# A decode kernel's w1 in one piece, and q's four products summed in the same rows

## The chip, the cores and the metric

The kernel runs on one core of a Trainium2 chip. The metric is the device time of one execution in microseconds, taken over several executions.

## The reference

Two layers, each of attention with a cached K and V and of a gated feed-forward, for four sequences with one token each. The same weights and the same cache serve both layers. Everything is 32 bit floating point.

```python
B, Sq, D = 4, 1, 512;  Hq, Hkv, Sk, Dh = 32, 8, 4096, 128;  F = 1792
def _A_ref(x, k_cache, v_cache, wq, wo):
    q = (x @ wq).reshape(B, Sq, Hq, Dh).transpose(0, 2, 1, 3)
    k, v = jnp.repeat(k_cache, 4, axis=1), jnp.repeat(v_cache, 4, axis=1)
    p = softmax(jnp.einsum("bhqd,bhkd->bhqk", q, k) * (Dh ** -0.5))
    o = jnp.einsum("bhqk,bhkd->bhqd", p, v)
    return o.transpose(0, 2, 1, 3).reshape(B, Sq, Hq * Dh) @ wo
def _B_ref(x, w1, w3, w2):
    return (silu(x @ w1) * (x @ w3)) @ w2
for _ in range(2):
    x = x + _A_ref(layernorm(x), A_k_cache, A_v_cache, A_wq, A_wo)
    x = x + _B_ref(layernorm(x), B_w1, B_w3, B_w2)
```

## The kernel before

All weights and the cache are laid out by the host as one long row per partition, `rows`, in the order in which the first layer uses them: output and query weights (`wo`, `wq`) of a group of heads, the tiles of K and V (`kv`) group by group, then `w1`, `w3` and `w2`. On the chip one buffer, `space`, has 218 units of 1 KB per partition. The table `LOADS` is written out by hand: each entry is (first unit in the stream, number of units, place in `space`). `pump` (L118) issues the entries strictly in order on SyncE's queue, and stops at the first entry whose place is still taken. `done` (L147) is called when a piece has been used for the last time; it frees the units and calls `pump`. So the use of a piece by TensorE is what lets a later load be issued. Some pieces are kept from the first layer for the second: all of `w1`, some `wq` and `wo`, and 28 of the 32 tiles of the last group of heads, with which the second layer begins.

A group of heads is one turn of the loop at the end of `tile_decode_layers`. `score` (L309) multiplies q with the K tiles of half the positions; the four sequences' products go to four blocks of 32 rows of one PSUM bank. Then `maximum` on VectorE, `exponent` on ScalarE, and `turn` (L343), which transposes the probabilities on TensorE. Between `maximum` and `turn`, TensorE forms the next group's q: `share_q` (L290). Its four products, one for each 128 rows of `wq`, go to four separate blocks of 32 rows of the bank `wide`; `take_q` scales all 128 rows; `turn_q` (L302), called from within the second `score`, multiplies each head's columns with `same`, which both adds up the four blocks and turns them: `misc[:, h * B:(h + 1) * B]` gets the head's q with the head dimension along the partitions. `copy_q` puts it into `qT`. `weigh` (L379) is the product with V. In all there are 15 calls of `share_q`; the first q of the second layer comes from `turn_over`.

The feed-forward (L452) has `gate` and `up` in two PSUM banks. The columns F = 1792 are cut into four blocks of 448, one for each 32 rows, and these into a first part of 256 columns, "a", and a second of 192, "b": both `w1` and `w3` are stored as an a-part and a b-part with four chunks of D each. `part` (L456) multiplies one such part, `swish` (L473) is the gate's sigmoid (ScalarE) and product (VectorE), `times_up` the product with `up` (VectorE), `turn_h` the transposes of h, and `down` (L497) the product with `w2`, whose result is added to x in `x_ps`. In the first layer the order is w3a, w1a, swish and times_up of a, w1b, first transposes, swish of b, w3b; in the second w1a, w1b, swish of all, w3a, times_up of a, w3b. `busy` and `hum` are matmuls of the identity that fill waits of TensorE.

A 32 bit matmul shows as two matmul and two weight load instructions in the trace, a transpose as one of each.

Of the kernel before, what the change touches and what calls it, by code (L numbers as in the profile page):

```python
# [8 lines left out]
F32 = mybir.dt.float32  # L9
AF = mybir.ActivationFunctionType  # L10
ALU = mybir.AluOpType
AX = mybir.AxisListType

B, D, HQ, HKV, SK, DH, F = 4, 512, 32, 8, 4096, 128, 1792
LAYERS = 2
REP = HQ // HKV
P = 128
KC = D // P
# [16 lines left out]
FJ = F // 4  # L35
HALF = 256
EPS = 1e-5
SCALE = DH ** -0.5
# [4 lines left out]
KB = 256  # L43
HOME = 8
SPACE = 218
TURN = HKV - 1
KEPT = (*range(2, 16), *range(20, 32))
HELD = 4
# [10 lines left out]
    (868, 8, 68), (876, 8, 186), (884, 8, 194), ("stash", 1, 202), (892, 8, 206), ("stash", 0, 214),  # L59
# [13 lines left out]
def tile_decode_layers(ctx: ExitStack, tc: tile.TileContext, rows, out):  # L73
    nc = tc.nc
    ctx.enter_context(tc.manual_schedule())
    const = ctx.enter_context(tc.tile_pool(name="const", bufs=1))
    work = ctx.enter_context(tc.tile_pool(name="work", bufs=2))
# [22 lines left out]
    for g in range(3, HKV):  # L100
        stream += tiles(g)
    stream += pair(6)
    for kind, n in (("w1a", KC), ("w1b", KC), ("w3a", KC), ("w3b", KC), ("w2", 14)):
        stream += [(kind, k) for k in range(n)]
    size = {"wq": HOME, "wo": HOME, "kv": U // KB, "w2": D // KB}
    for kind in ("w1", "w3"):
        size[kind + "a"], size[kind + "b"] = 4 * HALF // KB, 4 * (FJ - HALF) // KB
    offset, total = {}, 0
    for key in stream:
        offset[key] = total  # L110
# [34 lines left out]
        return place(where[key], size[key[0]])  # L145

    def done(layer, *key):  # L147
        if layer == 0 and (key[0][:2] == "w1" or key[0] in ("wq", "wo") and key[1] >= HELD or key[:2] == ("kv", TURN) and key[2] in KEPT):
            return
        at, n = where[key], size[key[0]]  # L150
        taken[at:at + n] = [False] * n
        pump()
# [4 lines left out]
    ident = const.tile([P, P], F32, name="ident")  # L157
    make_identity(nc, ident)
    same = const.tile([P, 32], F32, name="same")
# [3 lines left out]
    half, share, spare = columns[:, 0:2], columns[:, 2:3], columns[:, 3:4]  # L163
    rowsum, ssq, ve, rstd = columns[:, 4:5], columns[:, 5:6], columns[:, 6:8], columns[:, 8:10]
# [6 lines left out]
    part = work.tile([P, 32], F32, name="part", tag="p", bufs=1)  # L171
# [11 lines left out]
    x_ps, misc = sums_ps[:, 0, :], sums_ps[:, 1, :]  # L183
    wide = sums_ps.rearrange("p k c -> p (k c)")
# [18 lines left out]
    def hum(n):  # L203
        nc.tensor.matmul(sums_ps[:, 1:1 + n, :], ident, ident.unsqueeze(1).to_broadcast([P, n, P]),
                         start=False, stop=False)
# [73 lines left out]
        return xT, factor  # L279


    def copy_q(q=None):
        q = misc[:, 0:B * REP].rearrange("p (h b) -> p b h", h=REP) if q is None else q
        nc.vector.tensor_copy(qT[:, :, LEAD:].rearrange("p b (t r) -> p b t r", t=2)[:, :, :, 0:REP],
                              q.unsqueeze(2).to_broadcast([P, B, 2, REP]))

# [3 lines left out]
    def share_q(layer, g, xT):  # L290
        w = wq_of(g)
        for k in range(KC):
            nc.tensor.matmul(wide[32 * k:32 * k + 32, :], xT[:, 32 * k:32 * k + 32], w[:, k, :],  # L293
                             start=True, stop=True)
        done(layer, "wq", g)

    def take_q(rstd):
        shares = work.tile([P, REP * DH], F32, name="shares", tag="p", bufs=1)
        nc.vector.tensor_scalar(shares, wide, rstd, -D * SCALE, op0=ALU.mult, op1=ALU.mult)  # L299
        return shares  # L300

    def turn_q(shares):  # L302
        for h in range(REP):
            nc.tensor.matmul(misc[:, h * B:(h + 1) * B], shares[:, h * DH:(h + 1) * DH], same[:, 0:B],  # L304
                             start=True, stop=True)

# [142 lines left out]

    def feed_forward(layer, xT, factor):  # L452
        gate, up = o_ps if layer else o_ps[::-1]
        cols = {"a": slice(0, HALF), "b": slice(HALF, FJ)}

        def part(bank, kind, ks=range(KC)):  # L456
            s = cols[kind[2]]
            for k in ks:
                w = loaded(kind, k).rearrange("p (j f) -> p j f", j=4)
                for j in range(4):  # L460
                    nc.tensor.matmul(bank[32 * j:32 * j + 32, s], xT[:, 32 * k:32 * k + 32], w[:, j],  # L461
                                     start=(k == 0), stop=(k == KC - 1))
                done(layer, kind, k)

        def old_x():
            n = 1 if layer else KC
            nc.tensor.matmul(sums_ps[:, 0:n, :], ident, x_sb.unsqueeze(1).to_broadcast([P, n, P]), start=True, stop=False)

        h = work.tile([P, FJ], F32, name="h", tag="p", bufs=1)
        hT = work.tile([P, 14, B], F32, name="hT", tag="pT", bufs=1)  # L470
        pt = scores().rearrange("p (n s) -> p n s", n=NT)

        def swish(s):  # L473
            nc.scalar.activation(h[:, s], gate[:, s], AF.Sigmoid, scale=rstd[:, 0:1])
            nc.vector.scalar_tensor_tensor(h[:, s], gate[:, s], rstd[:, 0:1], h[:, s], op0=ALU.mult, op1=ALU.mult)

        def times_up(s):
            nc.vector.scalar_tensor_tensor(h[:, s], up[:, s], rstd[:, 0:1], h[:, s], op0=ALU.mult, op1=ALU.mult)

        def turn_h(u):  # L480
            if u == 0:
                for i in range(2):
                    nc.tensor.transpose(pt[:, i, :], h[:, i * P:(i + 1) * P], ident)
                nc.vector.tensor_copy(hT[:, 0:8, :],
                                      pt[:, 0:2, :].rearrange("p i (j b) -> p (i j) b", j=4)[:, :, 0:B])
            else:
                nc.tensor.transpose(pt[:, 2, :], h[:, 2 * P:3 * P], ident)
                nc.tensor.transpose(pt[:, 3, :], h[:, FJ - P:FJ], ident)
                nc.tensor.transpose(pt[0:64, 3, :], h[:, FJ - 64:FJ], ident)
                nc.vector.tensor_copy(hT[:, 8:12, :],  # L490
                                      pt[:, 2, :].rearrange("p (j b) -> p j b", j=4)[:, :, 0:B])
                last = pt[:, 3, :].rearrange("p (j u b) -> p j u b", j=2, u=2)
                for i in range(2):
                    nc.vector.tensor_copy(hT[64 * i:64 * i + 64, 12:14, :],
                                          last[64 * i:64 * i + 64, :, i, 0:B])

        def down():  # L497
            for m in range(14):
                t = loaded("w2", m)
                for k in range(KC):  # L500
                    nc.tensor.matmul(x_ps[32 * k:32 * k + B, :], hT[:, m, :], t[:, k * P:(k + 1) * P],  # L501
                                     start=False, stop=(m == 13))
                done(layer, "w2", m)
                if layer == 0 and m in (1, 3, 8, 11):
                    hum(1)
                if m == (1 if layer else 5):
                    turn_h(1)

        if layer == 0:
            part(up, "w3a", (0,))  # L510
            factor()
            part(up, "w3a", range(1, KC))
            old_x()
            part(gate, "w1a")
            swish(cols["a"])
            times_up(cols["a"])
            hum(3)
            part(gate, "w1b")
            turn_h(0)
            swish(cols["b"])  # L520
            nc.scalar.activation(spare, half[:, 0:1], AF.Exp)
            part(up, "w3b", (0, 1))
            hum(2)
            part(up, "w3b", (2, 3))
            times_up(cols["b"])
            hum(1)
        else:
            old_x()
            part(gate, "w1a", (0,))
            factor()  # L530
            part(gate, "w1a", range(1, KC))
            part(gate, "w1b")
            swish(slice(0, FJ))
            part(up, "w3a")
            times_up(cols["a"])
            part(up, "w3b")
            turn_h(0)
            times_up(cols["b"])
        down()

    for layer in range(LAYERS):
        order = orders[layer]
        if layer:
            xT, factor = turn_over(order[0][0])
        else:
            nc.vector.reduce_sum(rowsum, x_sb, axis=AX.X)  # L546
            xT, factor = layernorm()
# [6 lines left out]
        between = {1: factor} if layer else {}  # L554
        for n, (g, (first, last)) in enumerate(order):
# [10 lines left out]
            pT = turn(p)  # L566
            between = {}
            if n + 1 < len(order):
                shares = take_q(rstd[:, 0:1])
                between[2] = lambda shares=shares: turn_q(shares)  # L570
            if layer == 0 and n == TURN - 2:
                between[6] = lambda: center(TURN)
            if n > ready:
# [71 lines left out]
```

## Time and profile before

| | us |
|---|---|
| median of three executions | 703.92 (703.74 to 704.41) |
| profiled execution, its own time | 703.98 |
| its span | 702.2 |
| mean granted TensorE clock | 0.831 |

Busy time is the time in which an engine had at least one instruction of a group running; "mean ns" is the mean duration of one. Where instructions run side by side, the number times the mean is more than the busy time. The idle time behind a second bar is that of the engine just ahead of the group's instructions, with what ended it. In a timeline row the first number is the start and the second the duration, in us. For a DMA issue the last number is the median time from issue to landing, in us.

### The profile page before, as it was taken

What the parts mean: (1) busy time and instruction counts of PE and PEld (TensorE: products, weight loads), DVE (VectorE), ACT (ScalarE), POOL (GpSimd) and SP (SyncE); (2) the same over time, 40 slices, a digit from 0 to 9 for tenths busy, and PEclk for the clock granted to TensorE, in tenths of its full rate; (3) what the DMA queues carried; (4) which work ended last, traced back from release to release, by engine and by line L of the source; (5) the groups of instructions that cost most, each with busy time, mean ns of one, the idle gap of its engine ahead of it and who ended that gap; (6) DMA issues with size and microseconds to landing.
All of it is one profiled execution on the core that took longest, in us unless ns stands there. A gap on an engine that the chain in (4) does not pass through costs nothing.

```text
span 702.2 us, 7492 instructions
## 1 busy us (share of the span) xinstructions
PE 421.1 (60%) x3280; PEld 133.2 (19%) x3280; DVE 144.4 (21%) x512; ACT 41.7 (6%) x100; POOL 3.0 (0%) x10
## 2 busy tenths in 40 slices
PE   1266466444578409667687985745555744567676
PEld 0121121101112102121134221201111211111223
DVE  2012112121023103330221332112120211212231
ACT  0010000100001001010101210000100001000100
POOL 0000000000000000000000000000000000000000
PEclk9997677966769859886999998878977978779999
DMA  9999999999999999999999999999999999999996
GB/s 418 422 419 422 467 419 418 430 454 413 453 413 441 429 434 418 434 427 426 422 416 378 433 421 442 441 434 420 443 437 430 433 427 444 423 433 413 428 424 269
DMA packets 12271, 297.87 MB, mean 424 GB/s; under 512 B 1360, under 2 KB 1488, under 8 KB 4048
## 3 DMA queue, kind: packets, MB, share of 16 engines
q1 hardware_dynamic: 12240, 297.41, 99.0%
q8 instruction: 25, 0.41, 0.2%
q14 instruction: 6, 0.05, 0.0%
HBM read 297.34 MB, written 0.07 MB: 424 GB/s over the span
## 4 chain that ended last, share of the span: by engine, by line
DMA 73%; PE 23%; DVE 1%; another core or an unknown queue 1%; ACT 1%; issue 1%; SPq 0%; ACTq 0%; DVEq 0%
DMA space<-in_rows 73%; PE scores L320 11%; PE o L385 7%; PE sums_ps L304 1%; PE turned L346 1%; ACT p L339 1%; DVE acc L333 1%; PE scores L200 1%; PE stored L249 1%; PE o L461 0%; PE stored L439 0%; PE sums_ps L418 0%; PE sums_ps L429 0%; PE sums_ps L293 0%
## 5 line engine op out<-in xcount | busy, mean ns | idle before, releaser
L320 PE MATMUL scores<-space,qT 128*32 128x512 f32 x1024 | 166.7, 702 | 136.2 <-DMA space<-in_rows 135.5
L385 PE MATMUL o<-space,pT 128*16 128x512 f32 x1024 | 153.7, 713 | 102.7 <-DMA space<-in_rows 95.9
L320 PEld LDWEIGHTS scores<-space,qT 128*32 128x32 f32 x1024 | 35.5, 122 | 213.2 <-issue 174.2
L385 PEld LDWEIGHTS o<-space,pT 128*16 128x16 f32 x1024 | 31.7, 108 | 202.8 <-DMA space<-in_rows 98.0
L333 DVE TENSOR_REDUCE acc<-scores 128x1 f32<-128x512 f32 x32 | 22.1, 691 | 177.5 <-PE scores L320 177.5
L339 ACT ACTIVATE p<-scores,acc 128x512 f32<-128x512 f32 x30 | 20.6, 687 | 559.8 <-DVE acc L333 433.1
L408 DVE SCALAR_TENSOR_TENSOR o<-o,acc,o 128x128 f32<-128x128 f32 x112 | 39.3, 351 | 50.1 <-PE o L385 46.7
L348 DVE COPY pT<-turned 128x256 f32<-128x256 f32 x32 | 13.6, 424 | 161.9 <-PE turned L346 161.9
L346 PE MATMUL turned<-ident,p 128*128 128x128 f32 x128 | 22.7, 304 | 11.9 <-ACT p L339 11.9
L293 PE MATMUL sums_ps<-space,xT 128*32 128x512 f32 x120 | 23.5, 731 | 3.6 <-DMA space<-in_rows 3.6
L346 PEld LDWEIGHTS turned<-ident,p 128*128 128x128 f32 x128 | 14.7, 151 | 45.4 <-ACT p L339 25.8
L419 DVE COPY o<-sums_ps 128x16 f32<-128x16 f32 x16 | 2.8, 174 | 92.9 <-PE sums_ps L418 92.9
L304 PEld LDWEIGHTS sums_ps<-same,shares 128*128 128x128 f32 x120 | 15.6, 204 | 16.1 <-DVE shares L299 11.9
L304 PE MATMUL sums_ps<-same,shares 128*128 128x4 f32 x120 | 17.0, 265 | 0.9 <-DVE shares L299 0.9
L461 PE MATMUL o<-space,xT 128*32 128x192 f32 (+1 forms) x256 | 13.7, 355 | 3.1 <-DMA space<-in_rows 1.4
L439 PE MATMUL stored<-space,o 128*32 128x512 f32 x104 | 13.5, 592 | 0.0
L501 PE MATMUL sums_ps<-space,hT 128*4 128x128 f32 x224 | 9.1, 272 | 4.2 <-DMA space<-in_rows 3.5
L299 DVE TENSOR_SCALAR shares<-sums_ps,columns 128x512 f32<-128x512 f32 x15 | 11.1, 742 | 1.7 <-PE sums_ps L293 1.7
L209 PE MATMUL o<-columns,same 128*32 128x1 f32 x64 | 2.0, 181 | 14.5 <-DVE columns L546 13.5
L418 PEld LDWEIGHTS sums_ps<-columns,o 128*128 128x128 f32 x32 | 6.2, 240 | 20.3 <-issue 13.5
L461 PEld LDWEIGHTS o<-space,xT 128*32 128x32 f32 x256 | 7.8, 110 | 8.2 <-DVE xT L222 1.4
L418 PE MATMUL sums_ps<-columns,o 128*128 128x16 f32 x32 | 7.6, 315 | 0.6 <-DVE o L408 0.6
(101 smaller groups left out, 141.5 us busy)
## 6 DMA issues: line engine op xcount, KB each, us to landing
space<-in_rows SPq DMA_DIRECT2D x11, 4096.0 KB, 22.1
space<-in_rows SPq DMA_DIRECT2D x7, 2048.0 KB, 27.8
space<-in_rows SPq DMA_DIRECT2D x13, 1024.0 KB, 20.2
space<-in_rows SPq DMA_DIRECT2D x2, 6144.0 KB, 30.8
space<-in_rows SPq DMA_DIRECT2D x2, 5120.0 KB, 28.8
space<-in_rows SPq DMA_DIRECT2D x2, 4608.0 KB, 22.1
space<-in_rows SPq DMA_DIRECT2D x1, 7680.0 KB, 34.0
space<-in_rows SPq DMA_DIRECT2D x2, 3584.0 KB, 20.9
```

The source lines that it names most:

```text
L293: nc.tensor.matmul(wide[32 * k:32 * k + 32, :], xT[:, 32 * k:32 * k + 32], w[:, k, :], start=True, stop=True)
L304: nc.tensor.matmul(misc[:, h * B:(h + 1) * B], shares[:, h * DH:(h + 1) * DH], same[:, 0:B], start=True, stop=True)
L320: nc.tensor.matmul(ps[32 * b:32 * b + 32, :], qT[:, b, at:at + 32], t[:, i * BLOCK:(i + 1) * BLOCK], start=(m < 2), stop=(m >= TILES - 2))
L333: nc.vector.tensor_reduce(acc[:, i:i + 1], ps, axis=AX.X, op=ALU.max, negate=True)
L339: nc.scalar.activation(p.rearrange("p n s -> p (n s)"), ps, AF.Exp, bias=acc[:, i:i + 1], scale=1.0 if scale is None else scale, accum_out ...
L346: nc.tensor.transpose(pt[:, n, :], p[:, n, :], ident)
L348: nc.vector.tensor_copy(pT, pt.rearrange("p n (b r) -> p n b r", b=B)[:, :, :, 0:ROW])
L385: nc.tensor.matmul(o_ps[i][32 * b:32 * b + ROW, :], pT[:, r // 2, b, :], t[:, j * NB * DH:(j + 1) * NB * DH], start=(r < 2), stop=(r >= TI ...
L408: nc.vector.scalar_tensor_tensor(o, o_ps[s][:, j * DH:(j + 1) * DH], acc[:, 16 + NB * s + j:17 + NB * s + j], o, op0=ALU.mult, op1=ALU.add)
L418: nc.tensor.matmul(misc[:, 0:B * REP], o, head, start=True, stop=True)
L439: nc.tensor.matmul(bank[32 * h:32 * h + 32, :], oT[:, h, :], w[:, h, :], start=first, stop=last)
L461: nc.tensor.matmul(bank[32 * j:32 * j + 32, s], xT[:, 32 * k:32 * k + 32], w[:, j], start=(k == 0), stop=(k == KC - 1))
```

## The change

`w1` is stored as four whole chunks of 7 units instead of an a-part and a b-part; its two loads of 16 and 12 units become 21 and 7, at the same places. The first layer's feed-forward takes w1 whole, and its swish runs over all 448 columns; what follows is reordered. The four products of `share_q` are summed in PSUM in the first 32 rows; `take_q` scales 32 rows; `turn_q` turns each head with a transpose; `copy_q` reads with another stride.

```diff
-    (1180, 16, 146), (1152, 16, 0), (1168, 12, 16), (1196, 6, 140), (1202, 6, 146), (1208, 4, 158),
+    (1180, 16, 146), (1152, 21, 0), (1173, 7, 21), (1196, 6, 140), (1202, 6, 146), (1208, 4, 158),
...
-    for kind, n in (("w1a", KC), ("w1b", KC), ("w3a", KC), ("w3b", KC), ("w2", 14)):
+    for kind, n in (("w1", KC), ("w3a", KC), ("w3b", KC), ("w2", 14)):
...
-    def copy_q(q=None):
-        q = misc[:, 0:B * REP].rearrange("p (h b) -> p b h", h=REP) if q is None else q
+    def copy_q():
+        q = misc.rearrange("p (h b) -> p b h", h=REP)[:, 0:B, :]
...
-            nc.tensor.matmul(wide[32 * k:32 * k + 32, :], xT[:, 32 * k:32 * k + 32], w[:, k, :],
-                             start=True, stop=True)
+            nc.tensor.matmul(wide[0:32, :], xT[:, 32 * k:32 * k + 32], w[:, k, :],
+                             start=(k == 0), stop=(k == KC - 1))
...
-        nc.vector.tensor_scalar(shares, wide, rstd, -D * SCALE, op0=ALU.mult, op1=ALU.mult)
+        nc.vector.tensor_scalar(q, wide[0:32, :], rstd[0:32, :], SCALE, op0=ALU.mult, op1=ALU.mult)
...
-            nc.tensor.matmul(misc[:, h * B:(h + 1) * B], shares[:, h * DH:(h + 1) * DH], same[:, 0:B],
-                             start=True, stop=True)
+            nc.tensor.transpose(misc[:, 32 * h:32 * h + 32], q[:, h * DH:(h + 1) * DH], ident[0:32, 0:32])
...
-            part(gate, "w1a")
-            swish(cols["a"])
+            hum(3)
+            part(gate, "w1")
+            swish(cols["1"])
+            nc.scalar.activation(spare, half[:, 0:1], AF.Exp)
             times_up(cols["a"])
-            hum(3)
-            part(gate, "w1b")
+            part(up, "w3b", (0, 1))
             turn_h(0)
-            swish(cols["b"])
-            nc.scalar.activation(spare, half[:, 0:1], AF.Exp)
-            part(up, "w3b", (0, 1))
-            hum(2)
+            hum(1)
             part(up, "w3b", (2, 3))
             times_up(cols["b"])
             hum(1)
         else:
             old_x()
-            part(gate, "w1a", (0,))
+            part(gate, "w1", (0,))
             factor()
-            part(gate, "w1a", range(1, KC))
-            part(gate, "w1b")
-            swish(slice(0, FJ))
+            part(gate, "w1", range(1, KC))
+            swish(cols["1"])
```

More of the change, by code (lines that the diff above doesn't have):

```diff
@@ L102, in tile_decode_layers @@
     stream += pair(6)
-    for kind, n in (("w1a", KC), ("w1b", KC), ("w3a", KC), ("w3b", KC), ("w2", 14)):
+    for kind, n in (("w1", KC), ("w3a", KC), ("w3b", KC), ("w2", 14)):
         stream += [(kind, k) for k in range(n)]
     size = {"wq": HOME, "wo": HOME, "kv": U // KB, "w2": D // KB}
-    for kind in ("w1", "w3"):
-        size[kind + "a"], size[kind + "b"] = 4 * HALF // KB, 4 * (FJ - HALF) // KB
+    size["w1"], size["w3a"], size["w3b"] = F // KB, 4 * HALF // KB, 4 * (FJ - HALF) // KB
     offset, total = {}, 0
@@ L147, in done @@
     def done(layer, *key):
-        if layer == 0 and (key[0][:2] == "w1" or key[0] in ("wq", "wo") and key[1] >= HELD or key[:2] == ("kv", TURN) and key[2] in KEPT):
+        if layer == 0 and (key[0] == "w1" or key[0] in ("wq", "wo") and key[1] >= HELD or key[:2] == ("kv", TURN) and key[2] in KEPT):
             return
@@ L292, in share_q, with turn_q @@
         for k in range(KC):
-            nc.tensor.matmul(wide[32 * k:32 * k + 32, :], xT[:, 32 * k:32 * k + 32], w[:, k, :],
-                             start=True, stop=True)
+            nc.tensor.matmul(wide[0:32, :], xT[:, 32 * k:32 * k + 32], w[:, k, :],
+                             start=(k == 0), stop=(k == KC - 1))
         done(layer, "wq", g)
     def take_q(rstd):
[L298 to L302, printed above, removed]
+        q = work.tile([P, REP * DH], F32, name="shares", tag="p", bufs=1)[0:32, :]
+        nc.vector.tensor_scalar(q, wide[0:32, :], rstd[0:32, :], SCALE, op0=ALU.mult, op1=ALU.mult)
+        return q
+    def turn_q(q):
         for h in range(REP):
-            nc.tensor.matmul(misc[:, h * B:(h + 1) * B], shares[:, h * DH:(h + 1) * DH], same[:, 0:B],
-                             start=True, stop=True)
+            nc.tensor.transpose(misc[:, 32 * h:32 * h + 32], q[:, h * DH:(h + 1) * DH], ident[0:32, 0:32])
     def score(layer, g, c, between={}):
@@ L453, in feed_forward @@
         gate, up = o_ps if layer else o_ps[::-1]
-        cols = {"a": slice(0, HALF), "b": slice(HALF, FJ)}
+        cols = {"1": slice(0, FJ), "a": slice(0, HALF), "b": slice(HALF, FJ)}
         def part(bank, kind, ks=range(KC)):
-            s = cols[kind[2]]
+            s = cols[kind[-1]]
             for k in ks:
@@ L568, in tile_decode_layers @@
             if n + 1 < len(order):
-                shares = take_q(rstd[:, 0:1])
-                between[2] = lambda shares=shares: turn_q(shares)
+                q = take_q(rstd[:, 0:1])
+                between[2] = lambda q=q: turn_q(q)
             if layer == 0 and n == TURN - 2:
@@ L632 @@
     parts = [wog[0], wog[1], wqg[1], wqg[0], old.reshape(P, P), kv[0], *pair(2), kv[1], kv[2], *pair(4), *kv[3:], *pair(6),
-             *halves(w1), *halves(w3), full, rest]
+             chunks(w1), *halves(w3), full, rest]
     parts = [a.reshape(P, -1) for a in parts]
```

## The prediction

> **What bounds the kernel now.** I read the page first: busy shares, slices, queues, and the chain that ended last.
>
> ```profile
> PE 421.1 (60%) x3280; PEld 133.2 (19%) x3280; DVE 144.4 (21%) x512; ACT 41.7 (6%) x100; POOL 3.0 (0%) x10
> DMA  9999999999999999999999999999999999999996
> q1 hardware_dynamic: 12240, 297.41, 99.0%
> q8 instruction: 25, 0.41, 0.2%
> HBM read 297.34 MB, written 0.07 MB: 424 GB/s over the span
> DMA 73%; PE 23%; DVE 1%; another core or an unknown queue 1%; ACT 1%; issue 1%; SPq 0%; ACTq 0%; DVEq 0%
> ```
>
> TensorE is busy in 60% of the span; the 16 DMA engines have work in every slice but the last, and the load queue alone takes 99.0% of their time. The span is therefore a fixed 297.41 MB at the rate of the engines, plus a start and a tail. The 23% of the chain that fall to PE are not a second bound: the chain goes through the PE instruction that consumed a load, while the next loads were already moving. An edit to PE work changes the time only where it makes the queue run dry, where it lengthens the tail after the last landing, or where it changes the traffic itself.
>
> So the second reading is how far the queue runs ahead of the loads. These are issue-to-landing times: the first load of the kernel (the queue is empty), the usual large ones, and then the small ones of 350 to 400 us and of 370 to 382 us, where the first layer's feed-forward gives back its slots piece by piece.
>
> ```profile
> space<-in_rows SPq DMA_DIRECT2D x1, 4160.0 KB, 12.4
> space<-in_rows SPq DMA_DIRECT2D x11, 4096.0 KB, 22.1
> ...
> space<-in_rows SPq DMA_DIRECT2D x1, 3072.0 KB, 13.3
> space<-in_rows SPq DMA_DIRECT2D x7, 512.0 KB, 6.0
> ```
>
> 4160 KB at 424 GB/s are 10.0 us, so an unqueued load costs 2.4 us beside its bytes. A load of 4096 KB alone would take 9.9 + 2.4 = 12.3 us and takes 22.1: it can be issued 9.8 us later before an engine idles. For the 3072 KB load (units 908 to 932, the only one of that size between 350 and 400 us) this reserve is 13.3 - 7.4 - 2.4 = 3.5 us; for the 512 KB loads of 370 to 382 us it is 6.0 - 1.2 - 2.4 = 2.4 us. These three reserves are what every delay below is held against.
>
> The third reading is the tail.
>
> ```profile
> 670.64 15.79 SPq L138 DMA_DIRECT2D space<-in_rows  x7
> ...
> 697.54 1.71 PE L501 MATMUL sums_ps<-space,hT 128*4 128x128 f32 x32 [0.55 <-DMA space<-in_rows]
> 699.31 0.29 DVE L597 COPY space<-sums_ps 128x128 f32<-128x128 f32 x1 [5.01 <-PE sums_ps L501]
> 699.63 0.35 SPq L598 DMA_DIRECT2D out<-space  x1
> ```
>
> The last loads were issued by 686.4, and the w2 rows at 697.54 still wait for them: over 10 us of queue. After them come only a copy and the store. The change touches none of this.
>
> **The change part by part.** First q's products. `share_q` issues eight instructions of 128x512 (four products of two passes) in each of its 15 calls, `turn_q` eight of 128x4.
>
> ```profile
> L293 PE MATMUL sums_ps<-space,xT 128*32 128x512 f32 x120 | 23.5, 731 | 3.6 <-DMA space<-in_rows 3.6
> L249 PE MATMUL stored<-space,columns 128*128 128x512 f32 x8 | 3.7, 605 | 0.0
> L304 PE MATMUL sums_ps<-same,shares 128*128 128x4 f32 x120 | 17.0, 265 | 0.9 <-DVE shares L299 0.9
> L346 PE MATMUL turned<-ident,p 128*128 128x128 f32 x128 | 22.7, 304 | 11.9 <-ACT p L339 11.9
> ```
>
> 120 x 731 ns are 87.7 us, but the group is busy for 23.5: the four products, each in its own 32 rows, run side by side, and a call takes 1.57 us. Summed in the same rows they must follow one another. The nearest row is L249, also four products accumulated in one place: eight instructions in 3.7 us. The upper bound is 8 x 731 ns = 5.8 us. So a call costs 2.1 to 4.3 us more; I take 2.1, since L249 has the same lengths and order. `turn_q` falls from 17.0 / 15 = 1.13 us to four transposes. Those of L346, four times wider, take 22.7 / 32 = 0.71 us for four: 0.4 us less, perhaps 0.7. Net 1.4 to 3.9 us more per call, 21 to 59 us of PE in all. That is the sign opposite to the instruction count.
>
> The Trainium skill, page "TensorEngine Tiling (Array Packing)", section Theoretical Speedup, allows up to 4 times for a stationary side of at most 32 columns; here the trace shows 87.7 / 23.5 = 3.7 before, and the change gives it up. By that rule alone a call would cost 4 x 1.57 = 6.3 us, 4.7 us more, and 15 calls 71 us of PE.
>
> What hides it: the 9.8 us of reserve behind the large loads, in every group but one. PE is made late once per group and then waits again for a landing, so the delays do not add up; a group has 702 / 16 = 44 us, of which PE uses 26. The exception is the first group of the second layer, which runs on kept tiles.
>
> ```profile
> 388.52 1.04 PE L293 MATMUL sums_ps<-space,xT 128*32 128x512 f32 x8
> 390.77 0.66 PE L346 MATMUL turned<-ident,p 128*128 128x128 f32 x4 [1.21 <-ACT p L339]
> 393.19 1.05 PE L304 MATMUL sums_ps<-same,shares 128*128 128x4 f32 x8
> ```
>
> Here the call is 1.04 us and PE then waits 1.21 us for p. With 3.7 us the transposes of p start about 3.7 - 1.04 - 1.21 = 1.4 us later; 0.3 to 0.4 come back in `turn_q`. With 5.8 us it is 3.5. What is queued behind on PE are the second scores, whose last tiles release the 3072 KB load. 1.1 us late against 3.5 us of reserve costs nothing; at the upper bound, 3.2, still nothing.
>
> The multiplication and copy of q on DVE keep their column counts, and so their durations; fewer rows gain nothing that a row here shows. The column sums drop out with -D and `same`.
>
> Next, w1 in one piece. Bytes and number of loads stay. Only a boundary moves: 16 and 12 KB per partition become 21 and 7, issued by SP at the same two places. The first lands 5 x 128 KB / 424 GB/s = 1.5 us later, the second where it did.
>
> ```profile
> L461 PE MATMUL o<-space,xT 128*32 128x256 f32 x128 | 7.8, 381 | 1.3 <-DVE xT L222 1.1 <-DMA space<-in_rows 0.2
> L461 PE MATMUL o<-space,xT 128*32 128x192 f32 x128 | 6.2, 329 | 1.8 <-DMA space<-in_rows 1.2 <-DVE h L478 0.6
> 385.94 2.76 PE L320 MATMUL scores<-space,qT 128*32 128x512 f32 x24
> 368.90 1.51 PE L461 MATMUL o<-space,xT 128*32 128x192 f32 x32 [0.79 <-DMA space<-in_rows]
> 370.70 0.86 PE L461 MATMUL o<-space,xT 128*32 128x192 f32 x16
> 372.59 0.86 PE L461 MATMUL o<-space,xT 128*32 128x192 f32 x16 [0.40 <-DMA space<-in_rows]
> 373.94 0.62 PE L501 MATMUL sums_ps<-space,hT 128*4 128x128 f32 x16
> 377.21 0.40 PE L501 MATMUL sums_ps<-space,hT 128*4 128x128 f32 x8 [0.72 <-DMA space<-in_rows]
> ```
>
> Half of each L461 row is w1: (7.8 + 6.2) / 2 = 7.0 us in both layers. By L320 a 448 wide instruction is 2.76 / 24 x 448 / 512 = 0.10 us, and 64 of them are 6.4 us: 0.3 us less per layer, on a path that waits for landings.
>
> The order in the first layer matters more. Now both halves of the sigmoid and its product stand ahead of the first half's multiplication by up, and the last part of w3 comes right behind that. The second layer already runs so:
>
> ```profile
> 688.40 0.63 ACT L474 ACTIVATE h<-o,columns 128x448 f32<-128x448 f32 x1 [19.98 <-PE o L461]
> 689.07 0.68 DVE L475 SCALAR_TENSOR_TENSOR h<-o,columns,h 128x448 f32<-128x448 f32 x1 [3.16 <-ACT h L474]
> 690.05 0.48 DVE L478 SCALAR_TENSOR_TENSOR h<-o,columns,h 128x256 f32<-128x256 f32 x1 [0.29 <-PE o L461]
> 690.59 1.51 PE L461 MATMUL o<-space,xT 128*32 128x192 f32 x32 [0.61 <-DVE h L478]
> ```
>
> The last row says that w3's last columns wait until DVE has read the other columns of the same bank. So in the first layer: w1 ended at 370.4; the second load still lands just ahead of 368.90, and what follows it, one piece of eight instructions and the end of the one before, brings w1's end to about 369.9. Then 0.63 + 0.68 + 0.48 and about 0.2 of hand-overs give 371.9 for the first two pieces of w3b, which ran at 370.70: 1.2 us late. Queued behind it on PE are the transposes of h, the other two pieces, and w2, about 1.1 us late at 373.9; the two 512 KB loads and their neighbours that go into these slots are issued as late. Against a reserve of 2.4 us that is nothing, and at 377.21 PE waits for a landing again, so it is back on time. If the bank's wait did not occur, the delay would be 0; the bounds of this term on the time are 0 and, should the reserve be used up by the engine that runs ahead, 1 us. I take 0. The order of the filling matmuls changes inside these waits: nothing.
>
> In the second layer the feed-forward has 0.3 us less PE work ahead of w2, whose last loads are waited for: nothing. The loads that go into w1's first slot are issued about 0.3 us later, since its first piece is now 448 wide; against the 10 us of queue at the end that is nothing.
>
> Last, the traffic. 25 instruction packets took 0.2% of 16 x 702.2 us, about 22 us or 0.9 each (0.41 MB / 25 = 16 KB). Each holds one DMA engine while the others go on, so it delays the landings only if that engine is the last. 252 TensorE instructions fewer are about one packet: between 0 and 0.9 us less; spread over 16 engines 0.06. I take 0. That the remaining packets fall at other times, onto other moments of the queue, can move the end by one packet either way.
>
> **Sum.** 0 (q, hidden) + 0 (order, hidden) + 0 (w1) + 0 (packets) on the profiled execution's 703.98 us (span 702.2 and 1.8 around it), which is 0.06 above the median of the three times: 704.0 us. About 0.2%, or 1.4 us, is what a measurement of this kernel can tell from no change.
>
> **The rivals.** *Instruction packets make it faster.* The last DMA engine loses one or two packets that now fall on others: 0.9 or 1.8 us less, 702.2 for two. For it: the queue is never empty, so an engine's lost time is never won back but in the stretch of small loads. Against: only one packet in 25 goes. The Trainium skill, page "Runtime: NRT & Kernel Launch", section Instruction fetch mechanics, says that instructions come in blocks of 256, 16 KiB, through a DMA queue of the engine's own; the size of a packet here agrees.
>
> *The stretch of small loads runs dry, and it becomes slower.* The place is 371 to 377 us in the first feed-forward: w3b waits for DVE, the slots of w3b and w2 come free late. It decides from 2.4 us of delay on. My estimate is 1.2; were the hand-overs and the extra transposes double, 3.5 to 4, the loads would come 1.1 to 1.6 us late, and a packet on the wrong engine could add 0.9: 705.1 to 706.5 us. For it: this is the smallest reserve in the kernel, and it is a median, so single loads have less. Against: the landings re-time PE within 4 us.
>
> *The products do not serialize.* If one row group overlaps its own products after all, PE gets lighter; the time stays 704.0 because PE does not bound it.
>
> **How the numbers follow.** No change, with either behaviour of the products, 0.56. Faster by the packets 0.20. Slower by the dry stretch 0.24, for which the small reserve speaks. The range goes from two packets less to the dry stretch with 1.6 us: 702.2 to 705.6.
>
> **What would show it.** Right: the load queue again near 99.0%, the last w2 still waiting for DMA, L293's group near 55 us instead of 23.5 with its mean below 731 ns, the transposes of q below 11 us, 24 instruction packets. Wrong: a dip of the DMA digits or GB/s between 370 and 400 us well below those of before, loads of 512 KB that land in under 4 us from issue, or a w2 at the end that waits for PE.

## The result, and the profile after

The changed kernel takes 706.66 us (median of 17 executions, 704.43 to 711.6) against 703.92 us (17 executions, 703.54 to 704.62): ratio 1.0047, 95% interval 1.0032 to 1.0063. It is slower by about 3 us, and its times scatter over 7 us where the kernel before scatters over 1. Each ratio below is to the kernel before, run beside that experiment. In three of the experiments one execution took 1274 to 2196 us, in a slow state, and is left out of every figure. The profiled execution took 710.18 us (span 708.4), 3.5 us above its median; its differences from before are larger than the typical ones.

From the page of the changed kernel:

```profile
PE 451.1 (64%) x3156; PEld 131.5 (19%) x3156; DVE 144.2 (20%) x511; ACT 41.4 (6%) x99; POOL 3.0 (0%) x10
GB/s 418 414 415 470 415 419 446 432 422 438 426 433 432 442 419 424 438 426 426 414 419 353 368 423 431 443 449 414 431 455 415 434 434 421 449 433 406 425 423 224
q1 hardware_dynamic: 12240, 297.41, 98.4%
q8 instruction: 25, 0.41, 0.2%
HBM read 297.34 MB, written 0.07 MB: 420 GB/s over the span
DMA 69%; PE 27%; DVE 1%; another core or an unknown queue 1%; issue 0%; SPq 0%; ACT 0%; ACTq 0%
```

The same bytes went at 420 instead of 424 GB/s. The two slices with 353 and 368 lie between 372 and 407 us; before, the slices of this place had 378 and 433. There the load queue ran short; elsewhere the slices look as before.

The groups that the change touches (by line, shapes kept apart):

```profile
L292 PE MATMUL sums_ps<-space,xT 128*32 128x512 f32 x120 | 63.6, 681 | 3.4 <-DMA space<-in_rows 3.4
L303 PE MATMUL sums_ps<-ident,shares 32*128 32x32 f32 x60 | 6.4, 227 | 0.9 <-DVE shares L298 0.9
L459 PE MATMUL o<-space,xT 128*32 128x448 f32 x64 | 6.5, 542 | 2.1 <-DMA space<-in_rows 1.7 <-DVE xT L221 0.3
```

The products of q run one after another: 120 x 681 ns are 81.7 us for 63.6 of busy time, where before the ratio was 3.7. A call takes 4.2 us instead of 1.57.

The first feed-forward and the second layer's start, in the timeline:

```profile
366.96 3.21 PE L459 MATMUL o<-space,xT 128*32 128x448 f32 x32 [1.74 <-DMA space<-in_rows]
371.70 0.48 DVE L476 SCALAR_TENSOR_TENSOR h<-o,columns,h 128x256 f32<-128x256 f32 x1
372.24 0.86 PE L459 MATMUL o<-space,xT 128*32 128x192 f32 x16 [2.06 <-DVE h L476]
393.32 3.60 PE L292 MATMUL sums_ps<-space,xT 128*32 128x512 f32 x8
```

w1 now waits for its larger first load (366.96), and q's products in the second layer's first group take 3.60 us instead of 1.04. The first two pieces of w3b start at 372.24 instead of 370.70, behind VectorE's read of the same bank. The load that goes into their slots is issued later. These are the answers for the one 512 KB load issued there, of before (window from 371.4 us) and of after (window from 373.0 us):

```profile
space<-in_rows SPq DMA_DIRECT2D x1, 512.0 KB, 5.6
```

```profile
space<-in_rows SPq DMA_DIRECT2D x1, 512.0 KB, 4.1
```

Now the DMA digits of the window 370 to 382 us, 0.3 us each, of before and then of after:

```profile
DMA  8999999999899989997999999996887998999989
```

```profile
DMA  9999999999764996799999959799999999999999
```

Each digit is the busy share of the 16 engines in tenths. Before, the engines are nearly full through the stretch (lowest digit 6, at 378 us); after, there is a hole from 373.0 to 375.1 us, just where the refill is late. And by stretches (length; busy PE, PEld, DVE, ACT, POOL; granted clock; DMA share; GB/s), before first:

```profile
370.00:376.00 6.00, 5.39 (x86) 2.93 (x77) 0.94 (x3) 1.91 (x3) 0.00 (x0) 1.00 1.00 374
382.00:392.00 10.00, 7.64 (x125) 3.30 (x126) 3.16 (x12) 3.29 (x8) 0.70 (x1) 1.00 1.03 419
392.00:405.00 13.00, 12.48 (x108) 4.09 (x106) 5.24 (x22) 1.10 (x3) 0.00 (x0) 1.00 1.03 432
```

```profile
370.00:376.00 6.00, 3.94 (x68) 2.43 (x68) 1.78 (x4) 2.12 (x3) 0.00 (x0) 1.00 0.91 337
382.00:392.00 10.00, 8.87 (x106) 4.25 (x110) 1.77 (x8) 0.37 (x2) 0.70 (x1) 0.50 1.00 376
392.00:405.00 13.00, 13.00 (x94) 3.80 (x88) 3.56 (x11) 4.03 (x9) 0.00 (x0) 0.99 0.95 353
```

Three things went wrong in a row in this execution: the DMA hole at 373 us; a granted clock of 0.50 through 382 to 392 us; and a second hole behind it, 353 instead of 432 GB/s, in the second layer's first group, where TensorE waits for no load and its pace decides when slots come free. Which of them is the cause, the experiments had to say.

### The profile page after: what moved, and what is told of

It reads as the page before. It is cut to its first block, busy times and chain, and to the rows that moved or that the text cites. A ratio compares the mean times of both kernels' runs of the same rounds, so it can differ in the third digit from the quotient of the medians.

```text
span 708.4 us, 7238 instructions
## 1 busy us (share of the span) xinstructions
PE 451.1 (64%) x3156; PEld 131.5 (19%) x3156; DVE 144.2 (20%) x511; ACT 41.4 (6%) x99; POOL 3.0 (0%) x10
## 3 DMA queue, kind: packets, MB, share of 16 engines
q1 hardware_dynamic: 12240, 297.41, 98.4%
## 4 chain that ended last, share of the span: by engine, by line
DMA 69%; PE 27%; DVE 1%; another core or an unknown queue 1%; issue 0%; SPq 0%; ACT 0%; ACTq 0%
DMA space<-in_rows 69%; PE scores L318 11%; PE o L383 8%; PE sums_ps L292 4%; PE turned L344 1%; PE o L459 1%; PE stored L248 1%; PE sums_ps L303 1%; PE sums_ps L499 0%; DVE pT L346 0%; PE scores L259 0%; PE stored L437 0%; DVE o L406 0%; PE sums_ps L203 0%
## 5 line engine op out<-in xcount | busy, mean ns | idle before, releaser
L292 PE MATMUL sums_ps<-space,xT 128*32 128x512 f32 x120 | 63.6, 681 | 3.4 <-DMA space<-in_rows 3.4
L292 PEld LDWEIGHTS sums_ps<-space,xT 128*32 128x32 f32 x120 | 14.3, 124 | 48.1 <-issue 42.8
L459 PE MATMUL o<-space,xT 128*32 128x256 f32 (+2 forms) x192 | 13.4, 417 | 6.5 <-DMA space<-in_rows 3.3
L298 DVE TENSOR_SCALAR shares<-sums_ps,columns 32x512 f32<-32x512 f32 x15 | 10.9, 729 | 6.0 <-PE sums_ps L292 6.0
L459 PEld LDWEIGHTS o<-space,xT 128*32 128x32 f32 x192 | 5.8, 109 | 12.6 <-DVE h L476 4.9
L303 PEld LDWEIGHTS sums_ps<-ident,shares 32*128 32x128 f32 x60 | 4.8, 136 | 14.8 <-DVE shares L298 11.9
```

Of the source, the lines that this page charges most:

```text
L292: nc.tensor.matmul(wide[0:32, :], xT[:, 32 * k:32 * k + 32], w[:, k, :], start=(k == 0), stop=(k == KC - 1))
L303: nc.tensor.transpose(misc[:, 32 * h:32 * h + 32], q[:, h * DH:(h + 1) * DH], ident[0:32, 0:32])
```

## The experiments

At first I held the clock to be the cause, and q's serial products to be the rival. Unless another is named, "the hole" is the one from 373 us on.

**The w1 part alone.** Edit: the kernel before with the changed `LOADS`, stream and `feed_forward`, and the old `share_q`, `take_q`, `turn_q`, `copy_q`.

> Before, with the w1 part of the change alone (w1 in one piece, the new order of the first feed-forward); q's products stay in four row groups. Theory clock (the new order leaves TensorE idle in the first feed-forward, its clock falls to half around 382 us, and the first group of the second layer, which paces the loads, runs at half speed): some executions slower by 2 to 5 us, spread of the times over 2 us, median 705 to 706; a profile of a slow one shows clock 0.5 between 380 and 392 us. Theory serial q (the summed products make TensorE late in that group): 703.5 to 704.3 with the narrow spread of before, clock 1.0 in that stretch.

705.45 us (704.36 to 707.51), ratio 1.0026, interval 1.0016 to 1.0037. Over half of the loss is here, without any change to q. The clock was at 0.5 for only 3.4 us in this profile; the hole is there (window 370 to 382 us):

```profile
DMA  9999999875646977999989965799999999999999
```

**The q part alone.**

```diff
-            nc.tensor.matmul(wide[32 * k:32 * k + 32, :], ..., start=True, stop=True)
+            nc.tensor.matmul(wide[0:32, :], ..., start=(k == 0), stop=(k == KC - 1))
```

with the new `take_q`, `turn_q` and `copy_q`, and nothing of w1.

> Before, with the q part of the change alone (products summed in 32 rows, heads turned by transposes); w1 and the first feed-forward as before. Theory clock: 703.7 to 704.8, narrow spread, clock 1.0 between 360 and 420 us, the L293 group at some 60 us busy. Theory serial q: nearly all of the loss, 706 to 707, with DMA below 0.97 busy between 395 and 410 us.

703.96 us (703.51 to 711.35, one of eleven above 704.3), ratio 1.0008, interval 0.9989 to 1.0026. The profile is from a second run:

> The q part of the change alone once more, for a profile: 703.5 to 704.3; DMA digits of 370 to 382 us full, the L293 group at some 60 us busy with a mean below 731 ns, its transposes below 11 us.

704.04 us (703.5 to 706.88), ratio 1.0004, interval 0.9994 to 1.0015. TensorE is busier by 21 us, and that costs nothing that can be measured: the load queue hides it.

```profile
PE 442.1 (63%) x3220; PEld 130.9 (19%) x3220; DVE 144.3 (21%) x512; ACT 41.7 (6%) x100; POOL 3.0 (0%) x10
q1 hardware_dynamic: 12240, 297.41, 98.8%
```

The digits of 370 to 382 us were not quite as full as expected (one 6 among them).

**More filling matmuls ahead of the waits.**

```diff
-            hum(3)
+            for _ in range(3): hum(3)
             part(gate, "w1")
...
             times_up(cols["a"])
+            for _ in range(2): hum(3)
             part(up, "w3b", (0, 1))
```

> The changed kernel with two more filling matmuls ahead of w1 and two ahead of the first pieces of w3b, in waits of TensorE that are there anyway. Theory clock: the clock stays at 1.0 between 360 and 420 us, the spread closes to under 1.5 us, median 704 to 705. Theory serial q: as the changed kernel, 706 to 707.

706.16 to 711.7 us (five executions), ratio 1.0068, interval 1.0047 to 1.0089. Keeping TensorE busy in those waits does not help at all. In the profile, of the shortest execution, the hole is there with a clock of 1.00 from 370 to 376 us, as in the changed kernel; this speaks against the clock as the first cause. What the clock does behind the hole this run does not test, since it fell there all the same (0.85 from 382 to 392 us).

**The kernel before without the filling matmuls of the first feed-forward.** Edit: the three `hum` lines of `feed_forward` and the one in `down` taken out.

> The kernel before without the filling matmuls of the first feed-forward; the change is not in it. Theory clock: the clock falls in or behind the first feed-forward in many executions, 705 to 709, spread over 2 us. Theory serial q: no change, 703.5 to 704.5, since the loads pace that stretch whatever the clock.

703.84 us (703.52 to 706.88, one of twelve above 704.2), ratio 1.0000, interval 0.9992 to 1.0009. Yet the clock did fall, a third of the stretch from 382 us at half:

```profile
382.00:392.00 10.00, 7.68 (x108) 3.58 (x100) 2.62 (x10) 2.84 (x8) 0.70 (x1) 0.83 1.03 422
```

A short fall of the clock, with a full queue, cost nothing that can be measured. With that my first theory fell, as the start of the loss. The new one: the late refill at 373 us is the cause (the second rival of the prediction), whatever makes it late.

**One line moved in the changed kernel.**

```diff
             part(gate, "w1")
+            part(up, "w3b", (0, 1))
             swish(cols["1"])
             nc.scalar.activation(spare, half[:, 0:1], AF.Exp)
             times_up(cols["a"])
-            part(up, "w3b", (0, 1))
```

> The changed kernel with one line moved: the first two pieces of w3b stand ahead of the sigmoid, so that TensorE does not wait for VectorE's reads of the same bank. Theory dry (w3b's pieces run 1.3 us late, so their slots are refilled late, DMA engines that run ahead idle at 373 to 375 us, and q's longer products find the next loads with too little reserve): DMA digits of 370 to 382 us full again, the 512 KB load behind w3b issued near 371.7, median 703.6 to 704.6, spread under 1.5 us. Rival (the loss is from q's serial products and the clock in the second layer's first group): 706 to 707 as before the move.

704.13 us (703.5 to 708.05, two of eleven above 705.1), ratio 1.0011, interval 0.9998 to 1.0024. Timeline row, digits of 370 to 382 us, and stretch:

```profile
370.95 0.86 PE L459 MATMUL o<-space,xT 128*32 128x192 f32 x16 [0.93 <-DMA space<-in_rows]
```

```profile
DMA  9999999999989998999799999898999899999978
```

```profile
392.00:405.00 13.00, 12.48 (x105) 3.87 (x108) 5.77 (x23) 1.10 (x3) 0.00 (x0) 1.00 1.04 434
```

w3b again waits for its load and not for VectorE, the hole is gone, and so is most of the loss, with q still summed: the interval lies below that of the changed kernel. This is the strongest single test. One expectation missed: the times spread over 4.6 us instead of under 1.5. The profile is of a short execution (703.93 us), so what the two long ones did is not known.

**The w1 part alone, with the same line moved.**

> The w1 part of the change alone, with the first two pieces of w3b moved ahead of the sigmoid. Theory dry: no dip at 373 to 375 us, 703.6 to 704.4. Rival (w1 in one piece costs by itself, through its later first landing): 705 to 706 as without the move.

703.98 us (703.01 to 708.06, two of eleven above 705), ratio 1.0005, interval 0.9994 to 1.0016. w1 in one piece costs nothing that can be measured; the order did. It gains nothing either.

**The kernel before, with w3b made late**, in three doses of filling matmuls:

```diff
+            hum(2)                      # 0.55 us; hum(3) and hum(2) for 1.35 us; twice these for 2.7 us
             part(up, "w3b", (0, 1))
```

> The kernel before with 0.55 us of filling matmuls ahead of the first two pieces of w3b. If the reserve is the 2.4 us of my prediction, or the some 1 us that the engine furthest ahead has: no change, 703.7 to 704.3. If any delay costs: 704.3 to 705.

0.55 us: 703.87 us (703.5 to 704.52), ratio 0.9996, interval 0.9987 to 1.0005.

> The kernel before, with 1.35 us of filling matmuls put ahead of the first two pieces of w3b; nothing of the change is in it. Theory dry: as the w1 part alone, 705 to 706, times spread over 2 us, a dip of the DMA digits at 373 to 375 us. Rival: 703.7 to 704.3, since 1.35 us lies inside the reserve of 2.4 us and TensorE is kept busy.

1.35 us: 704.72 us (704.14 to 709.08), ratio 1.0017, interval 1.0005 to 1.0030.

> The kernel before with 2.7 us of filling matmuls ahead of the first two pieces of w3b, twice the earlier dose. With a reserve near 1 us (theory dry): 706 to 709. With a reserve of 2.4 us: 704 to 704.8.

2.7 us: 706.27 to 709.99 us, ratio 1.0049, interval 1.0035 to 1.0064. The digits of 370 to 382 us, dose by dose (the second profile is of a long execution, 708.16 us, the others of 704.52 and 706.27 us):

```profile
DMA  9989999997998989989975899999999999999999
```

```profile
DMA  9999999566749968997585899999999999999999
```

```profile
DMA  9999999986742232946899999878999999999999
```

The hole opens between the first dose and the second, and the time follows it. The longer doses made less delay than they last: the 512 KB load that refills w3b's first slots was issued at 371.59 us in the kernel before and 0.5, 1.1 and 2.3 us later in these profiles. So the reserve at this place lies between 0.5 and 1.1 us of delay, and a kernel in which nothing of the change stands loses time in the same way. The second dose cost 1.2 us by its ratio, less than the w1 part's 1.8, whose load was issued 1.3 us late; the intervals overlap.

**The q part with the 1.35 us dose.**

> The q part of the change alone, with the same 1.35 us of filling matmuls ahead of w3b. Theory dry: the two delays add in the second layer's first group: 706 to 708, as the changed kernel. If only the first dip counts: 705 to 706.

705.42 us (703.99 to 707.48), ratio 1.0020, interval 1.0011 to 1.0030. The two delays did not add up to the changed kernel's loss, and the result is not told apart from the dose alone.

**Filling matmuls behind the hole**, where TensorE waits for w2 in the changed kernel:

```diff
                 if layer == 0 and m in (1, 3, 8, 11):
                     hum(1)
+                if layer == 0 and m in (7, 10):
+                    hum(3 if m == 7 else 2)
```

> The changed kernel with filling matmuls in the waits of TensorE behind the dry stretch (three blocks after w2's row 7, two after row 10). Theory amplifier (the dry stretch makes TensorE wait, its clock halves for up to 10 us from 382 us on, and the second layer's first group, at half speed, releases its loads too late): the long half-clock stretch goes, the highest times with it, 705 to 706, spread under 2.5 us. If the clock is only a bystander: as the changed kernel, median near 706.7, times up to 711.

705.70 us (704.6 to 707.72), ratio 1.0031, interval 1.0019 to 1.0043. Its profile has the hole at 373 us, a clock of 1.00 from 382 to 392 and no second hole:

```profile
370.00:376.00 6.00, 3.93 (x41) 2.21 (x38) 1.57 (x4) 2.12 (x3) 0.00 (x0) 0.75 0.88 313
382.00:392.00 10.00, 8.84 (x125) 3.71 (x122) 2.62 (x10) 2.15 (x6) 0.70 (x1) 1.00 1.02 399
392.00:405.00 13.00, 12.48 (x96) 3.79 (x98) 4.38 (x19) 2.25 (x7) 0.00 (x0) 1.00 1.03 430
```

Its half clock, 3.4 us long, came earlier, from 373.0 us on. That is what the amplifier would do, but six executions do not separate 1.0031 from 1.0047, and the times spread over 3.1 us where I expected under 2.5.

**Does q add to the hole?** Three kernels on one chip. In the first, the products of the one call in the second layer's first group stay apart:

```diff
+            apart = layer == 1 and n == 0
-                share_q(layer, order[n + 1][0], xT)
+                share_q(layer, order[n + 1][0], xT, apart)
```

> The changed kernel, but the one call of q's products in the second layer's first group, the group that runs without waiting for loads, has the four row groups and the old turning; the other 14 calls are summed. If q's share of the loss arises in that group: as the w1 part alone, 705.4, with the load of 3072 KB issued 1 to 1.5 us earlier. If it arises in the other groups, or is not there: as the changed kernel in the same call, some 706.7, or all three alike.

706.38 us (705.35 to 711.45), ratio 1.0049, interval 1.0031 to 1.0068.

> The changed kernel once more, beside the others on one chip: median 706 to 707.5, times up to 711.

707.41 us (705.28 to 708.89), ratio 1.0048, interval 1.0035 to 1.0061.

> The w1 part alone once more, beside the others on one chip: median 705 to 706, at most 708. If q adds nothing on top of the dip, it is as the changed kernel.

705.95 us (704.6 to 708.32), ratio 1.0029, interval 1.0018 to 1.0039. Both times the whole change stands about 0.2% above its w1 part, with intervals that overlap a little. Keeping that one call's products apart brought no gain that can be measured, but its interval overlaps that of the w1 part too: a share of q through this call is neither shown nor excluded. The profile of this second run of the w1 part, one of its longer executions (706.43 us), shows the chain of hole, half clock and second hole without any change to q:

```profile
370.00:376.00 6.00, 3.94 (x73) 2.55 (x72) 1.78 (x4) 2.12 (x3) 0.00 (x0) 1.00 0.86 313
382.00:392.00 10.00, 8.87 (x106) 4.25 (x102) 1.77 (x8) 0.37 (x2) 0.70 (x1) 0.50 1.00 379
392.00:405.00 13.00, 11.79 (x97) 3.81 (x90) 3.57 (x11) 4.03 (x9) 0.00 (x0) 0.99 0.98 380
```

## Why the prediction was wrong

**The bound** was right: the load queue sets the time, 98.4% of the engines' span after, and TensorE's extra work by itself cost nothing that can be measured (the q part alone).

**q's products.** The mechanism was right, its size a little small: 4.2 us a call where I took 3.7 and bounded by 5.8; the transposes cost 6.4 / 15 = 0.43 us where I took 0.71. Net 2.0 us more per call, inside 1.4 to 3.9. The rule of the Trainium skill ("TensorEngine Tiling (Array Packing)", Theoretical Speedup) had the sign right, and with 4.7 us more a call too large a size against the 2.7 measured. The third rival, products that do not serialize, is out.

**w1 in one piece.** 6.5 us measured, 6.4 predicted, and with the line moved back it costs nothing that can be measured.

**The order of the first feed-forward** is the step that failed. The wait was named, and the bank's row in the second layer told of it; its length came out 1.5 us where I had 1.2. What was mis-sized is the reserve held against it: 2.4 us in the prediction, between 0.5 and 1.1 us by the doses. So the term of the sum that I put at 0, with 1 us as its bound, came to 1.8 us (the w1 part alone, 1.0026).

I had taken the time from issue to landing, less bytes and a fixed cost. But a load lands when the last of 16 engines is done, and the engines are not at the same place. Followed packet by packet in the trace of before, the engine furthest ahead was done with the load before the 512 KB load in question 0.9 us after that was issued, the one furthest behind 3.1 us after it. The kernel's very first load had its first packet 1.0 us after its issue. So the engine furthest behind had 2.1 us of reserve, near my 2.4, and the one furthest ahead had none: it came to the load early and idled for some 0.3 us already before the change. By these times, as an estimate, 0.5 us of delay leaves six of the 16 engines idle for a while, and 1.5 us twelve. A few engines that idle for some tenths of a microsecond did not show in the time, then. (The expectation for the smallest dose gives the engine furthest ahead some 1 us; the packets do not bear that out.)

The two quoted answers show the trap: issued 1.5 us later, that load landed 4.1 instead of 5.6 us after its issue, at the same moment, and by my measure nothing was lost, while the digits show other engines idle. I wrote that loads landing in under 4 us would prove me wrong; 4.1 with a hole shows that the sign was badly chosen, and the other one, the dip of GB/s between 370 and 400 us, was the good one.

Why engines that are ahead cost time in the end when they idle is argued and not shown: their lead would have paid for an instruction packet later on; without it, the packet delays the landings. In the packets of before, each instruction packet cost its engine some 1.5 us, and by 355 us the engines stood up to 3.3 us apart.

**The second rival** had the place, the mechanism and nearly the price (705.1 to 706.5 against 706.66), and got 0.24 because its threshold was set from that reserve. That its price came near is in part luck: it was worked out from a delay of 3.5 to 4 us, where 1.5 us was measured, and from a packet on the wrong engine, which no run shows. Its account lacked the second half, the half clock and the hole behind it.

**The first rival** is out: the profile after has 25 instruction packets as before, not 24, and the second profile of the same kernel has 24 and took 708.89 us, so that one packet fewer did not make it faster. By the Trainium skill's blocks of 256 instructions ("Runtime: NRT & Kernel Launch", Instruction fetch mechanics) some 250 instructions fewer would be about one packet; these two profiles show none fewer and one fewer.

**What stays open.** That a long half clock makes the loss larger fits the profiles and is not separated by a run. Of the ten profiled executions with the hole, four have 10.2 us of half clock from 382 to 384 us on; they took 706.43 to 710.18 us, with 353 to 389 GB/s from 392 to 405 us. The other six have 3.4 us of it and took 705.59 to 706.27 us, with 413 to 432 GB/s. The Trainium skill, page "TensorE: Matmul & The Clock Gate", Part 1, says that the clock halves by default and that activity in a free-running window of about 3.4 us releases it; a window that starts at another place in each execution would suit the scatter, but no run here shows that this is its source. Nor is it settled where q's share of 0.2% arises, if it is one. No version tried beats the kernel before.

## What to carry to other kernels

When a kernel is bound by its loads, look for the place where the smallest loads refill slots piece by piece, and judge every delay by the DMA digits of a narrow window, where engines that are ahead show as they run dry, and not by the time to the last landing, which shows the engine furthest behind. A matmul that was placed behind VectorE's read of another part of the same PSUM bank waited 2.06 us for it here; moving it one step ahead took most of the loss away. Large additions to an engine off the path (21 us of TensorE in the q part alone) can be free while 1.5 us in the wrong place is not.

## What was not expected of the hardware

A load's landing can hide a queue that has already run dry: the same landing at 377.2 us with and without a hole of 2 us in the digits. And with a delay of 1.5 us at one place the scatter between executions went from 1.1 us (before) to 7.2 us (after). The delay is not its only source: with the line moved back ahead and no hole in the profile, two of eleven executions still took about 708 us, and why is open.
